# A 2-D FFT and maxout layer: stage one's result turned by VectorE's 32x32 transposition instead of by a way through DRAM

## The chip, the cores and the metric

One core of a Trainium2 chip. The metric is the device time of one launch in microseconds (us). The inputs and the output are float32 in DRAM; the kernel's matmuls take bfloat16.

## The reference

```
x: (8, 3072, 256)             # 8 images
X = fft(x, axis=1); X = fft(X, axis=2); a = X.real          # (8, 3072, 256)
t = a.reshape(24576, 256)
h = max(t @ w1, t @ w2, t @ w3)                             # w1..w3: (256, 768)
out = h @ w_out                                             # w_out: (768, 256)
```

The real part of a 2-D FFT of a real image has a symmetry: row k and row 3072-k hold the same values with the second axis reversed. The kernel computes "even" and "odd" parts (`tE`, `tO`) for half of the rows and gets one row of each pair from their sum and the other from their difference. The second axis' DFT is folded into the weights: `gE`, `gO`, `gD` are products of w1 to w3 with tables of cosines and sines, made on the chip at the start.

## The kernel before

**Stage one** (`s`, L365). An image lies in `xt` as 49 residues s of the row index. 13 matmuls per image multiply it by a small table `tab`; seven evictions, mostly by ACT (L372, L376), put the result into `tb`: a partition is an output row of stage one (64 of them, two s in the two halves), and a residue's 128 columns lie side by side.

**The turn.** Stage two needs the residues on the partitions. `y` (L378) writes `tb` to a DRAM buffer `db`, and `z` (L388) reads it back as `yb`, 98 rows (two for each residue). Both go by SP's DMA queue. `u` (L393), `x0` (L396) and `c` (L403) make one extra column of `yb` from the image's first column.

**Stage two** (`k`, L406). 32 small matmuls an image multiply `yb` with the tables `te_tab` and `to_tab`; each group of 512 columns is evicted as a third of `tE` or `tO` (L413). The tables are sines of angles that VectorE reduces and ACT evaluates, in three parts of about 512 columns (`angle`, `table`).

**The units.** An image has 18 units: 3 blocks of 512 tokens times 6 slices of 128 hidden columns. A unit's `begin` makes the sum rows and its `finish`, one unit later, the difference rows. There are two kinds. In the plain kind (even units, and the first few odd ones) PE makes two products for the sum (L436, L437), ACT takes the relu of one bank (L450, `stmp`), VectorE the maximum with the other (L451, `hp`); then PE adds the difference product into the same banks (L444), and ACT and VectorE do the same again (`hm`). In the split kind (odd units from the seventh on) only one bank is kept: PE (L772, L773) and VectorE's maximum (L774, `hp`) with `plus3`, then PE's L444 and VectorE's L786 (`hm`) with `minus3`. `third` makes `plus3` and `minus3` a unit or more ahead: PE L756 and L758, ACT L760 (`odd`), VectorE L761 (`even`), POOL L765.

**The second layer** (`l2_block`, L464) runs ten steps a unit from a queue: matmuls into `po` (L460, L483), VectorE's add (L488, `ot`), stores by SP (L496) and by POOL's indirect DMA (L570).

**What sets the order.** All engines' queues are written by hand: instructions stand on each engine in program order. `plan` maps (image, unit) to a list of pieces, which stand at the end of that unit, after `l2_some(10)`. `ahead0` (image 0) and `ahead` (the others) say in which units the next image's pieces stand: the stage-one matmuls, `y`, `z`, `x`, `c`, and the groups `kE0` to `kO2`. Loads and mirrorings (`mirror`, L129, L131; `mirror_first`, L136) of images two ahead are in the same plan. PSUM: three banks for `ps_f`, two for `pse2`, one for `pse3`, two for `po`; a larger pool `ps_s` takes their place in the start.

**The start.** While image 0 arrives in four pieces, PE runs warm-up matmuls and stage one as far as it has data. Then come the weight products for the first three slices (`product`, L296: 16 matmuls of 384 columns), image 0's first stage-two groups, and unit 0. The weights come in six loads (`load_w`), three of them before the images and three after `z`.

Of the kernel before, what the change touches and what calls it, by code (L numbers as in the profile page):

```python
# [11 lines left out]
INT32 = mybir.dt.int32  # L12
AX = mybir.ActivationFunctionType
ALU = mybir.AluOpType

ROUND = 12582912.0
# [34 lines left out]
def kernel(  # L51
# [20 lines left out]
    KS = 2 * NS  # L72
# [8 lines left out]
    dbs = [d_pool.tile([NS, 4 * RI * 128], BF16, name=f"db{i}", tag=f"db{i}") for i in range(2)]  # L81
# [9 lines left out]
    x0u = consts.tile([128, KS + 1], BF16, tag="x0u")  # L91
    ybv = yb.rearrange("p (r e f) -> p r e f", e=2, f=128)
# [13 lines left out]
    gE = [consts.tile([128, DFF], BF16, name=f"gE{i}", tag=f"gE{i}") for i in range(2)]  # L106
    gO = [consts.tile([128, DFF], BF16, name=f"gO{i}", tag=f"gO{i}") for i in range(2)]
    gD = [consts.tile([128, DFF], BF16, name=f"gD{i}", tag=f"gD{i}") for i in range(2)]
# [41 lines left out]
    ang_r = gen.tile([128, 4 * RI], FP32, tag="ang_r")  # L150
    iota(ang_r, [[0, 4], [1, RI]], base=1)
    iota(ang_r.rearrange("p (g r) -> p g r", r=RI)[:, :, 15:17], [[0, 4], [16, 2]])
# [9 lines left out]
    def load_w(jh, after=None):  # L162
        for wsrc, wdst in ((moe_w1, w1_bf), (moe_w2, w2_bf), (moe_w3, w3_bf)):
            ld = nc.gpsimd.dma_start(
                out=wdst.rearrange("p (fc j) -> p fc j", fc=2)[:, :, jh * 384:(jh + 1) * 384],
                in_=wsrc.rearrange("(fc p) j -> p fc j", fc=2)[:, :, jh * 384:(jh + 1) * 384])
            if after is not None:
                tc.add_manual_dep(ld.ins, after.ins.name, AFTER, reason="others first")

    load_w(0)  # L170
# [3 lines left out]
    for r in (0, 6, 11):  # L174
        n = {0: 6, 6: 5, 11: 4}[r]
        iota(kv[:, r:r + n, :], [[1, n], [32, 96]], base=r + 1)
    iota(kvec[:, 1408:1504].rearrange("p (r j) -> p r j", r=2), [[16, 2], [32, 48]])
# [3 lines left out]
    rows_f = gen.tile([128, 12 * B], FP32, tag="rows_f")  # L181
    iota(rows_f.rearrange("p (b t u) -> p b t u", t=4, u=3), [[S, B], [-4, 4], [-1025, 3]],
         base=S - 1, cm=-32)
    zero = gen.tile([128, 512], BF16, tag="zero")
    nc.vector.memset(zero, 0.0)
    for db in dbs:
        pads = db[:, 64 * 128:].rearrange("s (r c) -> s r c", c=256)
        nc.sync.dma_start(out=pads, in_=zero[0:NS].rearrange("p (r c) -> p r c", c=256))
# [5 lines left out]
    ang_o = gen.tile([128, 4 * RI], FP32, tag="ang_o")  # L194
    nc.vector.memset(ang_o, 0.0)
    nc.vector.memset(ang_o[:, 0:RI], 8.0)
    nc.vector.memset(ang_o[:, 3 * RI:4 * RI], 24.0)
# [3 lines left out]
    def scal(out, in0, s1, op0, s2=None, op1=None, eng=None):  # L201
# [3 lines left out]

    up, sidx, hflag, alpha, sig, sgm = (small(n) for n in
                                        ("up", "sidx", "hflag", "alpha", "sig", "sgm"))
    scal(up, pidx, 64.0, ALU.is_ge)
    nc.vector.scalar_tensor_tensor(out=sidx, in0=up, scalar=-64.0, in1=pidx,
                                   op0=ALU.mult, op1=ALU.add)  # L210
    scal(hflag, sidx, 32.0, ALU.is_ge)
    scal(alpha, sidx, -2.0, ALU.mult, 31.0, ALU.add)
    nc.vector.scalar_tensor_tensor(out=alpha, in0=alpha, scalar=hflag, in1=sidx,
                                   op0=ALU.mult, op1=ALU.add)
# [3 lines left out]
    ang_q = gen.tile([128, 4 * RI], FP32, tag="ang_q")  # L218
# [4 lines left out]
    nc.vector.tensor_copy(out=tab[:, 0:64:2], in_=ang_q[:, 0:32])  # L223
    scal(tab[:, 1:64:2], ang_q[:, 0:32], sig, ALU.mult)
    scal(tabx, ang_q[:, 2 * RI:4 * RI], sgm, ALU.mult)

    dve = nc.vector.tensor_copy
    half = gen.tile([128, 256], FP32, tag="half")
    nc.vector.memset(half[:, 0:128], 64.0)
# [632 lines left out]
```

## Time and profile before

| | |
|---|---|
| median of 3 runs | 400.75 us (400.54 to 400.95) |
| the profiled execution: its own time, and its span | 400.15 us, 397.9 us |
| PE, DVE, ACT, POOL busy | 96%, 80%, 65%, 82% of the span |
| instructions of PE, DVE, ACT, POOL in the profile | 2739, 542, 466, 408 |
| DMA packets, bytes | 69532, 56.30 MB |
| granted TensorE clock | full, but for 14.0 to 20.8 us, where it was half |
| one image in the steady state | 45 us, 18 units |

How to read it: busy shares are means over stages with different limits. The first 40 us are the start, with PE idle in places; from there the table by windows gives PE as busy for 48.00 of 48 us. The lines of the profile are quoted with the prediction. In them DVE is VectorE, ACT is ScalarE, POOL is GpSimd, SP is SyncE, PE is TensorE's matmul and PEld its weight load; a duration that the timeline gives for one instruction overlaps with the next one's where instructions are pipelined, so the distance between starts can be shorter. `L774` is line 774 of the kernel before.

### The profile page before, as it was taken

The numbers are of one execution on the slowest core, as the hardware profiler recorded it, in microseconds if no ns is written. First come the engines' busy times: TensorE is split into PE (matmuls) and PEld (weight loads), VectorE is DVE, ScalarE is ACT, GpSimd is POOL, SyncE is SP. The second block draws the span as 40 slices with busy tenths as digits, with TensorE's granted clock in tenths as the row PEclk, the third lists the DMA queues.
The fourth block names the chain that finished last, engine by engine and source line by source line (L and its number), as shares of the span: only waits on it lengthen the run. The fifth ranks groups of instructions, "written<-read, shape, count | busy, mean of one in ns | idle before, by whom it ended". The sixth has DMA issues, their size and how long they took to land.

```text
span 397.9 us, 8345 instructions
## 1 busy us (share of the span) xinstructions
PE 382.8 (96%) x2739; PEld 236.3 (59%) x2739; DVE 317.6 (80%) x542; ACT 259.6 (65%) x466; POOL 324.6 (82%) x408
## 2 busy tenths in 40 slices
PE   7598999999999999999999999999999999999994
PEld 2254466656665666666665666666665666666673
DVE  6977797877887887877887887877887887887982
ACT  2577689768856788568866788568766547544420
POOL 7376389879988899889988899889878798879993
PEclk9799999999999999999999999999999999999999
DMA  8989987494776777395776877394432563322234
GB/s 121 196 175 195 167 229 147 122 192 145 141 154 123 177 165 162 108 190 148 147 155 117 183 166 153 108 200 127 129 112 82 133 154 104 91 77 50 88 88 138
DMA packets 69532, 56.30 MB, mean 141 GB/s; under 512 B 35040, under 2 KB 64992, under 8 KB 68292
## 3 DMA queue, kind: packets, MB, share of 16 engines
q0 software_dynamic: 23552, 26.53, 35.9%
q1 hardware_dynamic: 44898, 28.70, 28.1%
q10 hardware_dynamic: 1040, 0.56, 0.5%
q8 instruction: 21, 0.34, 0.4%
q14 instruction: 21, 0.17, 0.1%
HBM read 38.15 MB, written 31.71 MB: 176 GB/s over the span
## 4 chain that ended last, share of the span: by engine, by line
PE 86%; DMA 6%; ACT 3%; DVE 2%; POOL 1%; issue 1%; SPq 0%; POOLq 0%; DVEq 0%; ACTq 0%
PE po L460 30%; PE pse L444 11%; PE pse L436 7%; PE pse L437 7%; PE po L483 5%; PE pse L772 4%; PE pse L773 4%; PE e L756 4%; PE d L758 4%; PE ps L369 3%; DMA yb<-db 3%; PE ps L411 3%; PE pl L475 2%; DMA xt<-in_x_dram 2%; ACT stmp L450 1%; POOL xt L122 1%
## 5 line engine op out<-in xcount | busy, mean ns | idle before, releaser
L450 ACT ACTIVATE stmp<-pse 128x512 bf16<-128x512 f32 x150 | 89.6, 600 | 64.0 <-PE pse L444 39.8
L570 POOL DMA_INDIRECT out_dram<-ot,rows_m x92 | 102.3, 1112 | 17.9 <-issue 7.5
L765 POOL TENSOR_TENSOR plus<-even,odd 128x512 bf16<-128x512 f32 x69 | 87.9, 1274 | 34.0 <-DVE even L761 26.9
L765 POOL TENSOR_TENSOR minus<-even,odd 128x512 bf16<-128x512 f32 x69 | 87.6, 1270 | 0.0
L460 PE MATMUL po<-wout_bf,hp 128*128 128x256 bf16 x576 | 86.1, 273 | 0.0
L774 DVE SCALAR_TENSOR_TENSOR hp<-pse,plus 128x512 bf16<-128x512 f32 x69 | 47.6, 689 | 46.7 <-PE pse L773 26.2
L460 PE MATMUL po<-wout_bf,hm 128*128 128x256 bf16 x576 | 78.6, 273 | 0.0
L460 PEld LDWEIGHTS <-hp 128*128 128x128 bf16 x576 | 56.4, 98 | 26.1
L444 PE MATMUL pse<-tO,gD 128*128 128x512 bf16 x219 | 70.9, 379 | 0.0
L460 PEld LDWEIGHTS <-hm 128*128 128x128 bf16 x576 | 56.4, 98 | 16.3
L488 DVE TENSOR_TENSOR ot<-po,even 128x512 f32<-128x512 f32 x92 | 62.6, 681 | 0.0
L451 DVE TENSOR_TENSOR hp<-pse,stmp 128x512 bf16<-128x512 f32 x75 | 51.4, 685 | 10.8 <-ACT stmp L450 9.4
L436 PE MATMUL pse<-tE,gE 128*128 128x512 bf16 x150 | 56.8, 378 | 2.0 <-DVE hm L451 0.7
L451 DVE TENSOR_TENSOR hm<-pse,stmp 128x512 bf16<-128x512 f32 x75 | 51.5, 687 | 7.1 <-ACT stmp L450 3.9
L437 PE MATMUL pse<-tO,gO 128*128 128x512 bf16 x150 | 56.8, 379 | 0.0
L761 DVE SCALAR_TENSOR_TENSOR even<-vb,wcol,e 128x512 f32<-128x512 bf16 x69 | 50.8, 737 | 0.0
L786 DVE SCALAR_TENSOR_TENSOR hm<-pse,minus 128x512 bf16<-128x512 f32 x69 | 47.0, 681 | 0.9 <-PE pse L437 0.3
L760 ACT ACTIVATE odd<-d 128x512 f32<-128x512 f32 x69 | 41.3, 598 | 6.6 <-POOL minus L765 0.4
L129 ACT COPY xt<-xt 64x762 bf16<-64x762 bf16 (+1 forms) x48 | 40.2, 838 | 1.1
L372 ACT CAST tb<-ps 128x512 bf16<-128x512 f32 x46 | 24.8, 589 | 21.5 <-PE ps L369 21.5
L444 PEld LDWEIGHTS <-gD 128*128 128x128 bf16 x219 | 21.4, 98 | 23.1 <-issue 5.0
L483 PE MATMUL po<-gw,tO 128*128 128x512 bf16 x92 | 34.9, 380 | 0.0
(156 smaller groups left out, 468.3 us busy)
## 6 DMA issues: line engine op xcount, KB each, us to landing
yb<-db SPq DMA_DIRECT2D x7, 833.0 KB
xt<-in_x_dram POOLq DMA_DIRECT2D x14, 384.0 KB, 9.2
out_dram<-ot SPq DMA_DIRECT2D x55, 96.0 KB
out_dram<-ot SPq DMA_DIRECT2D x64, 64.0 KB
db<-tb SPq DMA_DIRECT2D x21, 192.0 KB
vb<-vd SPq DMA_DIRECT2D x23, 128.0 KB
xt<-in_x_dram POOLq DMA_DIRECT2D x7, 400.0 KB, 7.3
xt<-in_x_dram POOLq DMA_DIRECT2D x7, 368.0 KB
```

What stands on the lines that cost most here:

```text
L436: nc.tensor.matmul(pse[:, 0:n], gE[i][:, js], te, start=True, stop=False)
L437: nc.tensor.matmul(pse[:, 0:n], gO[i][:, js], to, start=False, stop=True)
L444: nc.tensor.matmul(pse, gD[i][:, js], to, start=False, stop=True, skip_group_check=True)
L450: nc.scalar.activation(out=stmp[:, 0:n], in_=pses[0][:, 0:n], func=AX.Relu)
L451: nc.vector.tensor_tensor(out=dst, in0=src3, in1=stmp[:, 0:n], op=ALU.max)
L460: nc.tensor.matmul(po, hcols(jc), wout_bf[:, jc * 256:(jc + 1) * 256], start=False, stop=(jc == NJC - 1), skip_group_check=True)
L483: nc.tensor.matmul(po, to[:, cp], gw[:, 256:768], start=True, stop=True)
L488: nc.vector.tensor_tensor(out=ot.rearrange("p (h c) -> p h c", h=2), in0=po.rearrange("p (h c) -> p h c", h=2), in1=lin.unsqueeze(1).to_br ...
L570: stored(nc.gpsimd.indirect_dma_start(out, bass.IndirectOffsetOnAxis(ap=rows_m[0:128 - lo, at_row: at_row + 1], axis=0), ot[lo:128, 256:51 ...
L761: nc.vector.scalar_tensor_tensor(out=even3, in0=vb, scalar=wcol[:, jc:jc + 1], in1=e3, op0=ALU.mult, op1=ALU.add)
L765: nc.gpsimd.tensor_tensor(out=dst, in0=even3, in1=odd3, op=op)
L774: nc.vector.scalar_tensor_tensor(out=dst, in0=pse2, scalar=0.0, in1=sums[g][0], op0=ALU.max, op1=ALU.max)
```

## The change

- **The turn.** `tb` becomes a tile of 32-bit words, each a pair of bf16 columns, with 64 pairs x 32 residue slots. ACT's evictions write pairs 128 bytes apart. `t` transposes blocks of 32x32 words on VectorE from `tb` into `yb`, whose words of one residue slot lie 256 bytes apart when written: image 0 in one instruction of 128x64x32, the others in four of 128x16x32 (`t0` to `t3`). `y`, `z`, the DRAM buffers and their padding are gone.
- **Rows renumbered.** The turn gives each quadrant of 32 partitions 16 rows of `yb`; stage two uses 17. The seventeenth comes out in the sixteenth row of the neighbouring quadrant, and `f` puts it right, twice (for two pairs of quadrants): ACT copies 32 x 256 bf16 across, and VectorE's memset clears the place that it came from. Stage two's matmuls take 128 rows for 98 (unused residue slots are zero).
- **The extra column.** `x0` writes `yb` directly for images 1 to 7, so `c` is used for image 0 alone, in parts; `u` is two copies on POOL for one.
- **The plan.** `ahead0`: `t0` to `t3` at units 8 to 11, `f` behind `t3`, `x` at 12. `ahead`: `t0` to `t3` at units 4, 6, 8, 10, `f` behind `t3`, `x` at 11.
- **The start.** The first weights come in three loads of 128 columns and three of 256; the last three no longer wait for `z`. The first products are 16 matmuls of 128 columns in one bank and 16 of 256 columns in two banks, before 16 of 384; one eviction takes a bank. Part of the angle reduction goes from VectorE to ACT (`turns`) and POOL, and the tables 512:1024 move to units 0 and 1 of the plan.

```diff
-    tb = consts.tile([128, 25 * 128], BF16, tag="tb")
-    tbv = tb.rearrange("p (s f) -> p s f", f=128)
-    yb = consts.tile([128, 2 * RI * 128], BF16, tag="yb")
+    tb = consts.tile([128, 64 * 32], UINT32, tag="tb")
+    tbw = tb.rearrange("p (f s) -> p f s", s=32)
+    tbv = tb.bitcast(BF16).rearrange("p (f s l) -> p f s l", s=32, l=2)
+    yb = consts.tile([128, 2 * RI * 64], UINT32, tag="yb")
+    ybw = yb.rearrange("p (q f) -> p q f", f=64)
+    ybv = yb.bitcast(BF16).rearrange("p (r e f) -> p r e f", e=2, f=128)
...
-    load_w(0)
...
+    load_w(0, 0, 128)
+    ramp(0)
+    load_w(1, 0, 128)
+    ramp(6)
+    load_w(2, 0, 128)
+    for k in range(3):
+        load_w(k, 128, 384)
...
+    def turns(q, v, per):
+        nc.scalar.activation(out=q, in_=v, func=AX.Identity, scale=1.0 / per, bias=rnd[:, 0:1])
+        nc.scalar.activation(out=q, in_=q, func=AX.Identity, scale=1.0, bias=rnd[:, 1:2])
...
-                evict(out=tb[:, k * 512:(k + 1) * 512], in_=ps1)
+                evict(out=tbv[:, :, 4 * k:4 * k + 4, :],
+                      in_=ps1.rearrange("p (s f l) -> p f s l", s=4, l=2))
...
-        def y(self, s0=0, s1=NS, second=nc.sync):
...
-        def z(self, i0=0, i1=RI, s0=0, s1=NS):
...
+        def t(self, f0=0, f1=64):
+            nc.vector.transpose(out=ybw[:, 0:32, f0:f1].rearrange("p q f -> p f q"),
+                                in_=tbw[:, f0:f1, :])
+
+        def f(self):
+            for a in (0, 64):
+                nc.scalar.copy(out=ybv[a:a + 32, 16], in_=ybv[a + 32:a + 64, 15])
+                nc.vector.memset(ybw[a + 32:a + 64, 30:32, :], 0)
...
-            nc.scalar.copy(out=x0s[0:KS, :], in_=psx[0:KS, 0:RI])
+            nc.scalar.copy(out=out, in_=psx[:, 0:RI])
...
-                nc.tensor.matmul(ps2[:, c0:c0 + wd], ybv[0:KS, i, which, :],
-                                 tab[0:KS, g * 512 + c0:g * 512 + c0 + wd], start=True, stop=True)
+                nc.tensor.matmul(ps2[:, c0:c0 + wd], ybv[:, i, which, :],
+                                 tab[:, g * 512 + c0:g * 512 + c0 + wd], start=True, stop=True)
...
     m.s(4, pool=ps_s)
-    m.s(5, pool=ps_s)
+    table(0, 0, 512)
+    m.s(5, pool=ps_s, evict=dve)
     m.s(6, pool=ps_s)
-    m.y(32, NS, nc.scalar)
...
+    m.t()
     m.u()
-    m.x0()
-    tables(0, 512)
-    m.z(0, 6, 0, 32)
...
+    m.x0(x0s)
+    table(1, 0, 512)
+    psg0 = products(ps_f, 0, 2, 0, 128)
+    keep(psg0, 0, 2, 0, 128, nc.scalar.copy)
+    table(2, 0, 512)
+    for k in range(3):
+        load_w(k, 384, 768)
...
+    psg1 = products(ps_s, 0, 1, 128, 384)
     warm_up(2)
+    psg2 = products(ps_s, 1, 2, 128, 384)
+    m.c(0, 6)
+    differ(0, 2, 0, 128)
     m.k(0, 0, dve)
-    keep_product(psg, 1, 1, 0, dve)
-    m.c(0, 6, nc.scalar.copy)
     m.k(1, 0)
-    table(2, 512, 1024)
...
-    for (u, fn) in ((0, lambda: next(second)), (0, lambda: m.c(6, RI, nc.scalar.copy)),
+    for (u, fn) in ((0, lambda: wrap(512, 1024)), (0, lambda: next(second)),
+                    (0, lambda: m.c(6, 15)), (0, lambda: differ(0, 2, 128, 384)),
+                    (0, lambda: table(1, 512, 1024)), (0, lambda: table(2, 512, 1024)),
+                    (1, lambda: table(0, 512, 1024)), (2, m.f), (2, lambda: m.c(15, RI)),
...
-    ahead = {1: ("s0", "s1"), 2: ("s2", "y0", "s3", "s6"), 3: ("s4", "s5", "y1", "u"), 5: ("x",),
-             7: ("z",), 11: ("c",), 12: ("kO0",), 13: ("v0", "kE0", "kO1"), 14: ("v1", "kE1"),
-             15: ("kO2",), 16: ("v2", "kE2", "end")}
+    ahead = {1: ("s0", "s1"), 2: ("s2", "s3", "s6"), 3: ("s4", "s5", "u"), 4: ("t0",), 6: ("t1",),
+             8: ("t2",), 10: ("t3", "f"), 11: ("x",), 12: ("kO0",), 13: ("v0", "kE0", "kO1"),
+             14: ("v1", "kE1"), 15: ("kO2",), 16: ("v2", "kE2", "end")}
```

More of the change, by code (lines that the diff above doesn't have):

```diff
@@ L12 @@
 INT32 = mybir.dt.int32
+UINT32 = mybir.dt.uint32
 AX = mybir.ActivationFunctionType
@@ L270, in angle @@
             nc.vector.tensor_tensor(out=kvec[:, cs], in0=kvec[:, cs], in1=q[:, cs], op=ALU.add)
-    def angles(c0, c1):
-        for part in range(2):
-            angle(part, c0, c1)
     def table(k, c0=1024, c1=NHALF + 1):
@@ L284, in table, with product @@
                                  bias=half_pi)
-    def tables(c0, c1):
-        for k in range(3):
-            table(k, c0, c1)
-    def product(i, half, jh, pool, tag):
-        psg = pool.tile([128, 512], FP32, name="psg", tag=tag)
+    def product(psg, c, i, half, j0, j1):
         hs = slice(half * 128, (half + 1) * 128)
@@ L315, in prep_first @@
             for half in range(2):
-                keep_product(product(i, half, 1, ps_f, "ps"), i, half, 1, nc.vector.tensor_copy)
+                psg = ps_f.tile([128, 512], FP32, name="psg", tag="ps")
+                product(psg, 0, i, half, 384, 768)
+                (nc.vector.tensor_copy, nc.scalar.copy)[half](
+                    out=g_all[:, 2 * i + half, 384:768], in_=psg[:, 0:384])
+                if half:
+                    differ(i, i + 1, 384, 768)
                 yield
@@ L406, in k, with c @@
+        def c(self, i0=0, i1=RI):
+            nc.scalar.copy(out=ybv[:, i0:i1, 1, 0], in_=x0s[:, i0:i1])
         def k(self, which, g, evict=nc.scalar.copy):
@@ L599 @@
     m.s(1, pool=ps_s)
-    m.y(0, 16)
     warm_up(5)
```

212 lines of the change are left out of this document (105 added, 107 removed).

## The prediction

> **What bounds the kernel now.** First the page's busy rows and slices.
>
> ```profile
> PE 382.8 (96%) x2739; PEld 236.3 (59%) x2739; DVE 317.6 (80%) x542; ACT 259.6 (65%) x466; POOL 324.6 (82%) x408
> PE   7598999999999999999999999999999999999994
> PEclk9799999999999999999999999999999999999999
> ```
>
> PE is full from slice 4 (about 40 us) to the last. The table by windows makes it exact:
>
> ```profile
> 22.30:42.00 19.70, 17.55 (x150) 9.99 (x151) 15.01 (x28) 13.40 (x29) 13.99 (x25) 1.00 1.10 175
> 90.00:138.00 48.00, 48.00 (x347) 30.01 (x345) 38.73 (x62) 35.66 (x64) 42.43 (x51) 1.00 0.69 148
> 186.00:234.00 48.00, 48.00 (x347) 29.94 (x345) 38.84 (x61) 35.97 (x63) 42.54 (x50) 1.00 0.72 155
> ```
>
> (columns: window, its length, busy PE, PEld, DVE, ACT, POOL, clock, DMA). PE's waits after 42 us are three, 0.9 us in all, none on the way through DRAM: L411, which reads `yb`, waits there 0.2 us, for ACT. So for images 1 to 7 the DRAM way is hidden, and removing it can't gain. It is seen only for image 0, in the chain of waits:
>
> ```profile
> 15.46 3.71 DMA db<-tb
> 19.52 2.63 DMA yb<-db
> 22.28 0.40 PE ps L411 x6
> ```
>
> Yet PE itself waited only 0.34 us there: until 21.9 it ran the weight products (L296) and the warm-ups, half of them at half clock (granted 0.5 from 14.0 to 20.8, two steps of 3.4).
>
> The steady state then hangs on slack. VectorE and ACT are each other's and PE's partners in every unit; this is the place that decides (an odd unit's `hp`, L774, in image 3; the same gap within 0.02 us in images 1 to 6):
>
> ```profile
> 189.91 0.68 DVE L451 TENSOR_TENSOR hp<-pse,stmp 128x512 bf16<-128x512 f32 x1
> 190.51 0.68 DVE L488 TENSOR_TENSOR ot<-po,even 128x512 f32<-128x512 f32 x1
> 191.11 0.68 DVE L774 SCALAR_TENSOR_TENSOR hp<-pse,plus 128x512 bf16<-128x512 f32 x1
> 191.71 0.68 DVE L451 TENSOR_TENSOR hm<-pse,stmp 128x512 bf16<-128x512 f32 x1
> 192.22 0.82 ACT L129 COPY xt<-xt 64x762 bf16<-64x762 bf16 x1
> 192.43 0.38 PE L444 MATMUL pse<-tO,gD 128*128 128x512 bf16 x1
> ```
>
> L444 adds into the bank that L774 reads, so it can't begin before L774 ends, 191.79: slack 0.64. On VectorE, steps of 512 follow each other every 0.60 us.
>
> **Start-up, part by part.** (1) Image 0's two DMAs leave the path: 3.71 + 2.63 and their issue (15.28 to 22.28) go. In their place: mirrors and the stage-one eviction to about 15.9, small VectorE steps, one transposition of 2,048 words a partition. At VectorE's contiguous f32 rate (512 elements every 0.60) that is some 2.2 us, 16.75 to about 19.0; at double, to 21.1. (2) PE's own queue is next late: s5, s6 and psx to 15.85, psg0 (16 matmuls of 128 columns at half clock, 0.107 each by L296's 0.32 for 384) to 17.55, psg1 to 19.26, two warm-ups to 20.1, psg2 to 21.3. So k starts near 21.35 in place of 22.28: -0.9, whether the transposition takes 2.2 or 4.4. PE's stage-one work is the same and 16 more short matmuls cost 0.1. The narrower loads cost 0: the chain shows no weight load, and PE has stage one to run until 15.85; each us that the first one lands later than that would cost one. The SP queue loses 42 issues that PE never waited for. (3) Back comes ACT's order. The 512:1024 tables now stand in unit 0, after unit 0's relu and before unit 1's:
>
> ```profile
> 23.44 0.72 ACT L283 ACTIVATE to_tab<-q,half_pi 128x512 bf16<-128x512 f32 x1
> 24.71 0.69 DVE L451 TENSOR_TENSOR hp<-pse,stmp 128x512 bf16<-128x512 f32 x1 [1.08 <-ACT stmp L450]
> 26.01 0.69 DVE L451 TENSOR_TENSOR hp<-pse,stmp 128x512 bf16<-128x512 f32 x1
> ```
>
> Before, unit 1's hp starts 2.56 after unit 0's first matmul (23.45). After: hp (0.60), `wrap` (0.70), |angle| (0.61), to_tab (0.72), unit 1's relu (0.60) follow each other across the two engines, 4.45: +1.9, with `f` and `c` of image 0 +0.2; PE has nothing else to do there (17.55 of 19.7). Start in all: -0.9 + 2.1 = +1.2 (bounds -0.7 if the clock rises one 3.4 us window earlier and the tables hide, +1.4 without that).
>
> **Steady state.** (4) y, z (33 + 11 DMAs) and `c` removed: 0, hidden now. PE in k: 128 rows for 98, same columns: 0. (5) Added per image: four chunks of 512 words, at 0.60 each, in units 4, 6, 8, 10. VectorE's 38.8 of 48 (36.4 of an image's 45.15) becomes 39: room in the mean. t0, t1 and t2 stand ahead of L774 of units 5, 7, 9, which have idle time plus slack of 1.1, 1.7, 1.6: 0. (6) t3 and `f` stand in unit 10, exactly ahead of the L774 shown, where VectorE has no idle time. `f` is copy (ACT), memset (VectorE), copy, memset: the copies wait for t3, each memset for its copy, and L774 and hm (L451) queue behind the memsets. t3 191.11 to 191.80; a copy of 256 on ACT, 0.185 + 256 x 0.84 ns by the slope of L129's two lengths = 0.40: first to 192.2, second to 192.6; memset to 192.7; L774 192.74 to 193.43. L444 192.43 becomes 193.46: PE stalls 1.03 us, with no other work in its queue ahead of that matmul. Six images (2 to 7): 6.2 us. (7) For image 1 the pieces lie in units 8 to 11 of image 0: t1 and t2 are 1.2 ahead of unit 11's L774 with about 1.0 of room: 0.25; t3 and `f` stand before `ot` and before hm (L786, 58.72), which frees the bank for unit 13's matmul at 59.93; t3, both copies and the memsets take about 1.9 more: 1.7 of it stalls. Together 2.0.
>
> **The unknown: strided words.** Evictions now write bf16 pairs 128 bytes apart, the transposition words 256 bytes apart; the trace has neither. Lower bound: contiguous price, 0.589 an eviction and 0.60 a chunk. Upper bound, from ACT's copies to bf16 at 512 bytes' stride:
>
> ```profile
> L404 ACT COPY yb<-x0s 98x17 bf16<-98x17 bf16 x7 | 1.9, 265 | 1.1 <-DMA yb<-db 1.0
> L136 ACT COPY xt<-xt 64x49 bf16<-64x49 bf16 x6 | 2.5, 409 | 0.1
> ```
>
> 32 elements more cost 0.144: 4.5 ns an element for 0.84 contiguous. At 4.5 a pair, an eviction is 1.33 us, and 12 of them put ACT from 33.6 to 42.5 of 45.15 us an image. At 4.5 a word a chunk is 2.4 us, VectorE 46.6 of 45.15: bound by VectorE. I take the contiguous price, as whole 4-byte words are nearer to the f32 rows of VectorE than to single bf16; both ends stay for the range. [...]
>
> **Sum**, against the profiled execution's 400.15: +1.2 + 2.0 + 6.2 = 409.5. The median of the runs is 0.6 above it: 410.1, said as 410.
>
> **Rivals.**
> A, strided words cost double or more (slower still). At 1.2 a chunk t0 to t2 eat the slack of units 5, 7 and 9 and t3 adds 0.55: about 2.0 an image for 1.03, image 1 3 us: near 417. If instead ACT's pairs cost 1.33, some 2 us an image more: 423. Both: about 430; the full 4.5 ns on VectorE, beyond 440. For it: the two ACT rows; against: they are 2-byte elements. Chance 0.32. [...]
> B, `f` is hidden (the copies are so short that the chain ends by 192.43): then only the start is left, 400.75 + 1.2, about 402. Against: the order of the queues and the slack of 0.64. Chance 0.10.
> C, faster: the start gains and nothing is given back. It needs the 512:1024 tables to hide beside PE's L411 and products, and a chain of t3 and `f` below 0.64 us. Then k at 21.35 or, if the clock is back by 17.4, at 19.5: -0.9 to -2.5, 398.3 to 399.9. For it: all DMA is off image 0's path; against: unit 0's ACT queue has 1.3 us put in it. It holds from the point where L774 of unit 11 ends by 192.43. Chance 0.10.
> D, no difference: gains and losses cancel. Chance 0.02.
> The forecast, 406 to 413 alone: 0.46.
>
> The range leaves out most of C, half of B and A's upper quarter: 402 to 427. About 0.2% (0.8 us) is what a measurement of this kernel can tell from no change; faster 0.10, same 0.02, slower 0.88.
>
> **What would show it.** Right: PE waits at L444 in units 11 of images 1 to 6, each about 1 us, for DVE hp; two small memsets ahead of it on VectorE, waiting for ACT's yb copies; transposition rows of 0.65 to 0.7 us; tb evictions near 0.59; k(0,0) near 21.4; unit 1's hp 4.4 after unit 0's first matmul. Wrong: PE still 48.00 of 48 in every window; chunk or eviction rows of 1.2 us and more, which make A; PE waits at e or `po` for POOL or ACT, which I have not priced.

## The result and the profile after

The changed kernel takes 421.31 us (median of 6 runs, 419.83 to 423.23); the kernel before, run beside it, 400.64. Ratio 1.052, 95% interval 1.0486 to 1.0548: slower by 20.7 us, where +9.3 was forecast. The profiled execution took 422.2 us with a span of 420.4 (before: 400.15 and 397.9).

The page's busy rows and slices of the kernel after:

```profile
PE 388.8 (92%) x2755; PEld 239.3 (57%) x2755; DVE 348.8 (83%) x588; ACT 265.5 (63%) x478; POOL 330.9 (79%) x422
...
PE   7668997999899998999899998999899998999994
PEclk9698998999999999999999999999999999999999
```

The row of 9s of before is broken by an 8 about every image, and slices 2, 3 and 7 are low (a slice is 10.5 us). The table by windows of the kernel after (columns as before: window, length, PE, PEld, DVE, ACT, POOL, clock, DMA):

```profile
90.00:138.00 48.00, 46.16 (x332) 28.50 (x332) 40.33 (x63) 33.85 (x61) 40.50 (x49) 1.00 0.51 109
186.00:234.00 48.00, 46.18 (x333) 28.81 (x332) 41.10 (x66) 34.30 (x62) 40.41 (x49) 1.00 0.52 109
```

PE, 48.00 of 48 before, now lacks 1.8 in each. No other engine is full, so it waits for steps in an order.

The loss by stage follows from two kinds of marks in PE's timeline: the first `psw` matmul (end of the start) and the one-column matmul that closes stage two of each image.

| stage | before | after | loss |
|---|---|---|---|
| to `psw` | 38.83 | 43.58 | 4.75 |
| to the end of image 1's stage two | 34.06 | 38.87 | 4.81 |
| the next six images, to the last mark | 267.31 | 280.02 | 12.71 |
| of these, one image in the steady state | 44.88 | 47.06 | 2.18 |

The three losses make 22.3 of the 22.5 by which the spans differ. The medians differ by less, 20.7, as the profiled execution of the kernel after is 0.9 above its median and that of before 0.5 below its own.

Two of these losses hang in part on the execution that was profiled. Three kernels of the experiments (the one without `f` and the first two plans) have the same code up to `psw`, and theirs stands at 42.50 to 43.46: the start loses 3.7 to 4.75. And 1.7 of image 1's 4.81 is a stretch at half clock that four kernels with the same work in image 1 don't show (below).

**The new instructions.** The groups by shape of the kernel after (count, busy, mean ns of one, idle before it):

```profile
L415 DVE STREAM_TRANSPOSE yb<-tb 128x512 uint32<-128x512 uint32 x28 | 29.6, 1057 | 0.0
L415 DVE STREAM_TRANSPOSE yb<-tb 128x2048 uint32<-128x2048 uint32 x1 | 3.7, 3724 | 0.1
L406 ACT CAST tb<-ps 128x512 bf16<-128x512 f32 x45 | 24.3, 588 | 16.5 <-PE ps L403 16.5
L420 ACT COPY yb<-yb 32x256 bf16<-32x256 bf16 x16 | 6.4, 402 | 16.8 <-DVE yb L415 16.6
L421 DVE MEMSET yb<- 32x128 uint32 x16 | 2.6, 165 | 5.6 <-ACT yb L420 2.9 <-issue 2.6
```

A chunk takes 1.06 us, and its successor starts 0.91 us behind it (190.47 to 191.38 below), not 0.60: 1.74 ns a word (the difference of the two lengths over 1,536 words). The pair-wise eviction costs what the contiguous one did (588 ns, before 589), and `f`'s copy the 0.40 that was worked out.

**An odd unit 11.** The timeline of the kernel after in image 3 (start, duration; in brackets idle time and its releaser), the place that the prediction showed for before:

```profile
205.55 1.05 DVE L415 STREAM_TRANSPOSE yb<-tb 128x512 uint32<-128x512 uint32 x1
...
206.64 0.83 ACT L420 COPY yb<-yb 32x256 bf16<-32x256 bf16 x2 [2.31 <-DVE yb L415]
...
207.12 0.17 DVE L421 MEMSET yb<- 32x128 uint32 x1 [0.52 <-ACT yb L420]
...
207.55 0.17 DVE L421 MEMSET yb<- 32x128 uint32 x1 [0.26 <-issue]
207.74 0.69 DVE L808 SCALAR_TENSOR_TENSOR hp<-pse,plus 128x512 bf16<-128x512 f32 x1
...
208.49 0.38 PE L476 MATMUL pse<-tO,gd_all 128*128 128x512 bf16 x1 [1.41 <-DVE hp L808]
```

(L808 is before's L774, L476 its L444.) t3, copy, memset, copy, memset, L808, L476 stand in the order forecast. From the start of t3 to that of L808 it is 2.19 us; the prediction's steps give 1.63. PE's wait is 1.41 as the profile counts it, from the modelled end of the matmul ahead.

**Unit 9**, in which the prediction put no stall. The same timeline from unit 4's t0 on:

```profile
190.47 1.06 DVE L415 STREAM_TRANSPOSE yb<-tb 128x512 uint32<-128x512 uint32 x1
...
192.56 0.72 DVE L795 SCALAR_TENSOR_TENSOR even<-vb,wcol,e 128x512 f32<-128x512 bf16 x1
...
193.43 1.27 POOL L799 TENSOR_TENSOR plus<-even,odd 128x512 bf16<-128x512 f32 x1 [1.51 <-DVE even L795]
...
197.37 2.56 POOL L602 DMA_INDIRECT out_dram<-ot,rows_m  x1 [0.21 <-issue]
...
199.98 1.28 POOL L799 TENSOR_TENSOR plus<-even,odd 128x512 bf16<-128x512 f32 x1
...
201.30 0.69 DVE L808 SCALAR_TENSOR_TENSOR hp<-pse,plus 128x512 bf16<-128x512 f32 x1 [0.70 <-POOL plus L799]
...
202.04 0.38 PE L476 MATMUL pse<-tO,gd_all 128*128 128x512 bf16 x1 [0.40 <-DVE hp L808]
```

Each of these steps is compared with the same step of the kernel before, whose timeline has

```profile
178.11 0.74 DVE L761 SCALAR_TENSOR_TENSOR even<-vb,wcol,e 128x512 f32<-128x512 bf16 x1
...
185.54 1.27 POOL L765 TENSOR_TENSOR plus<-even,odd 128x512 bf16<-128x512 f32 x1
...
186.85 0.69 DVE L774 SCALAR_TENSOR_TENSOR hp<-pse,plus 128x512 bf16<-128x512 f32 x1 [1.59 <-POOL plus L765]
...
187.60 0.38 PE L444 MATMUL pse<-tO,gD 128*128 128x512 bf16 x1
```

PE's matmul ahead of it (L806 of unit 7, before's L772) is 13.89 us later than before (194.54 for 180.65). But `even` is later by 14.45 (178.11 before), the first `plus` by 14.43 (179.00), the second by 14.44 (185.54), L808 by 14.45 (186.85), L476 by 14.44 (187.60). So t0 puts VectorE 0.56 us behind PE, POOL's first `plus` waits for `even` and then has no room: `plus`, `minus`, two scatters and the next `plus` follow each other until 201.3. The 1.59 us in which VectorE was idle before L774 there were a wait for this chain; PE had no slack at its end (L774 at 186.85 ended 0.06 before L444 began). t1 (195.01) and t2 (199.54) stand in idle time of units 7 and 9, and no step that PE waits for begins behind them: they cost nothing.

From unit 9 to unit 11 the shift grows to 16.06 (L476 at 208.49, before's L444 at 192.43). So unit 9 loses 0.55 and unit 11 1.62, the 2.17 of an image's 2.18.

**Image 1.** The table of PE's waits of the kernel after, from 46 to 400 us (sum, times, longest):

```profile
PE pse L476 <- DVE hp L808: 11.0, 12, 1.4
...
PE pse L806 <- DVE hm L820: 2.6, 2, 2.3
```

The twelve are those of units 9 and 11 in images 2 to 7. The two on L806 belong to image 1's pieces: 0.27 at 60.49 and 2.30 at 67.83, where `hm` stands behind t3, `f` and `ot`, as step 7 said. The long one leaves 1.10 us of PE work in a window of 3.4 us, and the next one runs at half clock. The table by windows of the kernel after, in the start and here:

```profile
27.00:30.40 3.40, 1.79 (x14) 0.90 (x13) 2.33 (x6) 3.16 (x6) 3.03 (x8) 1.00 1.51 238
30.40:33.80 3.40, 3.35 (x15) 1.66 (x15) 3.32 (x5) 2.05 (x5) 3.40 (x6) 0.54 1.28 175
...
64.60:68.00 3.40, 1.10 (x11) 0.81 (x9) 2.59 (x6) 2.54 (x5) 3.25 (x3) 1.00 0.35 64
68.00:71.40 3.40, 3.40 (x13) 1.75 (x12) 2.41 (x4) 2.08 (x5) 2.39 (x6) 0.53 0.73 126
```

In the window at half clock PE's matmuls of 512 columns start 0.43 us apart (L790 at 69.13, L792 at 69.56), at full clock 0.22 (L468 at 63.81, L469 at 64.03), so 3.4 us there do 1.7 us of work: about 1.7 of image 1's 4.81 is this. The runs bear it out: the kernels with the evictions on ACT, with the angle step moved, with the start's new order and with the first plan have the same work in image 1 and no half clock there, and take 37.17 to 37.19 us for it, 1.7 less than 38.87. The gap in front is the same (the two waits sum to 2.6 in each), so the window at half clock is in part luck: in steps of 3.41 us counted from the clock's changes, the gap lies in one step here and is shared by two with the angle step moved (lines with that experiment). The other 3.1 are the change's.

**The start.** The timeline of the kernel after:

```profile
18.45 3.72 DVE L415 STREAM_TRANSPOSE yb<-tb 128x2048 uint32<-128x2048 uint32 x1
...
22.23 0.40 PE L443 MATMUL ps<-te_tab,yb 128*128 128x96 bf16 x6 [0.39 <-DVE yb L415]
...
23.27 1.28 DVE L333 CAST g_all<-psg 128x512 bf16<-128x512 f32 x2
...
24.61 0.39 PE L468 MATMUL pse<-tE,g_all 128*128 128x512 bf16 x1 [1.73 <-DVE g_all L333]
...
30.91 1.19 DVE L212 TENSOR_SCALAR kvec<-kvec,s_of,phi 128x513 f32<-128x513 f32 x1
```

The transposition begins at 18.45, not 16.75, and takes 3.72, so k(0,0) stands at 22.23, where it stood before (22.28): nothing gained in this execution. VectorE's last mirroring of image 0 ends at 16.12 here, behind angle steps and a memset, and at 13.96 before; in the three kernels with the same code up to `psw` k(0,0) stands at 21.17 to 22.09. VectorE's evictions of the products come behind it, so unit 0's first matmul (L468) is at 24.61 for 23.45, and unit 1's `hp` at 29.10 for 26.01. Then VectorE's angle step (L212) takes 1.19, which was 0.54 before; POOL is at its mirror copies at that time (28.70 to 31.8; before they began at 34.29). The half-clock window above follows.

### The profile page after: what moved, and what is told of

It reads as the page before. It is cut to its first block, busy times and chain, and to the rows that moved or that the text cites. A ratio compares the mean times of both kernels' runs of the same rounds, so it can differ in the third digit from the quotient of the medians.

```text
span 420.4 us, 8330 instructions
## 1 busy us (share of the span) xinstructions
PE 388.8 (92%) x2755; PEld 239.3 (57%) x2755; DVE 348.8 (83%) x588; ACT 265.5 (63%) x478; POOL 330.9 (79%) x422
## 4 chain that ended last, share of the span: by engine, by line
PE 62%; DVE 16%; issue 9%; POOL 8%; ACT 2%; DMA 1%; DVEq 0%; POOLq 0%; ACTq 0%
PE po L492 21%; PE pse L476 9%; PE pse L468 5%; PE pse L469 5%; PE po L515 3%; PE pse L806 3%; POOL plus L799 3%; DVE hm L483 3%; POOL out_dram L602 3%; PE pse L807 3%; PE ps L403 3%; DVE yb L415 3%; PE ps L443 2%; PE d L792 2%; PE e L790 2%
## 5 line engine op out<-in xcount | busy, mean ns | idle before, releaser
L476 PE MATMUL pse<-tO,gd_all 128*128 128x512 bf16 x219 | 71.7, 384 | 11.1 <-DVE hp L808 11.0
L808 DVE SCALAR_TENSOR_TENSOR hp<-pse,plus 128x512 bf16<-128x512 f32 x69 | 47.4, 686 | 31.6 <-PE pse L807 18.1
L483 DVE TENSOR_TENSOR hp<-pse,stmp 128x512 bf16<-128x512 f32 x75 | 51.3, 684 | 12.4 <-ACT stmp L482 11.4
L468 PE MATMUL pse<-tE,g_all 128*128 128x512 bf16 x150 | 56.8, 379 | 3.5 <-DVE g_all L333 1.7
L469 PE MATMUL pse<-tO,g_all 128*128 128x512 bf16 x150 | 57.0, 380 | 0.0
L476 PEld LDWEIGHTS <-gd_all 128*128 128x128 bf16 x219 | 21.4, 98 | 23.2 <-issue 5.3
```

The lines of the kernel that those rows point to most:

```text
L468: nc.tensor.matmul(pse[:, 0:n], gE[i][:, js], te, start=True, stop=False)
L469: nc.tensor.matmul(pse[:, 0:n], gO[i][:, js], to, start=False, stop=True)
L476: nc.tensor.matmul(pse, gD[i][:, js], to, start=False, stop=True, skip_group_check=True)
L483: nc.vector.tensor_tensor(out=dst, in0=src3, in1=stmp[:, 0:n], op=ALU.max)
L808: nc.vector.scalar_tensor_tensor(out=dst, in0=pse2, scalar=0.0, in1=sums[g][0], op0=ALU.max, op1=ALU.max)
```

## The experiments

The theory: (a) words 256 bytes apart cost 1.74 ns each, which makes the chunks long; (b) t3 and `f` hold up L808 of unit 11; (c) the chunks put VectorE late, which reaches PE through POOL's `plus` in unit 9; (d) the start's 4.75 is VectorE's order. The rivals: the stalls come from the mere presence of chunks, from the new order of ACT's tables, or from other waits that the profile puts down to L808.

Short words, all else the same. `yb`'s words are written side by side, so stage two reads other data:

```diff
-            nc.vector.transpose(out=ybw[:, 0:32, f0:f1].rearrange("p q f -> p f q"),
+            nc.vector.transpose(out=yb[:, 0:2048].rearrange("p (f q) -> p f q", q=32)[:, f0:f1, :],
```

> The changed kernel with the transposition's output words side by side instead of 256 bytes apart (the words then lie at wrong places; same number of words, same plan). Theory (the words' distance costs): the chunk of 512 words falls from 1.06 us to about 0.68, image 0's 2,048 words from 3.72 to about 2.2. Then t1 fits into the 0.70 us that VectorE is idle ahead of unit 7 and the wait in unit 9 (0.57 us by the start of L476) is gone, and the one in unit 11 falls from 1.58 to about 1.1: 2.18 an image becomes 1.0 to 1.2, which is what the prediction had; with image 1 some -7 to -8: 413 to 414.5. Rival (a transposition of 32-bit words takes two cycles a word wherever it writes): rows stay at 1.06 and the time at 421.

416.00 us, ratio 1.038 (1.0347 to 1.0413). The groups of this kernel:

```profile
L415 DVE STREAM_TRANSPOSE yb<-tb 128x512 uint32<-128x512 uint32 x28 | 19.6, 701 | 0.0
L415 DVE STREAM_TRANSPOSE yb<-tb 128x2048 uint32<-128x2048 uint32 x1 | 2.3, 2311 | 0.1
```

The same words cost 1.05 ns each when written side by side, 1.74 when 256 bytes apart. The image goes from 47.06 to 46.41: the words' distance is worth 0.65 an image, and 5.3 us in all by the medians (4.3 by the profiled spans). Unit 9's wait falls from 0.40 to 0.16, unit 11's from 1.41 to 1.07: both hang on the chunk's length. The forecast's own price for a chunk (0.60 between starts) was this kernel's (0.62). Even so an image loses 1.53 against before, more than the 1.0 to 1.2 expected here and than the 1.03 of the forecast.

Without `f` (the seventeenth row of `yb` is not put right in images 1 to 7):

```diff
-            mm.f()
+            pass
```

> The changed kernel without f (the two ACT copies and two VectorE memsets) for images 1 to 7; the 17th row is left out there. Theory (t3 and f together hold L808 of unit 11): the wait in unit 11 falls from 1.58 us to about 0.4 (t3 alone, 1.0 for 0.64 of slack), unit 9's 0.57 stays: images 2 to 7 gain 6 x 1.15 = 6.9; image 1's 2.3 us wait at unit 13 loses about 1 us, and with a gap shorter than a clock window the half-speed window behind it (1.7 us) goes too: about 411 to 412.5. Rival (the long transposition holds the queue by itself, f runs in its shadow): within 1 us of 421.

410.85 us, ratio 1.0257 (1.0219 to 1.0294); the image 45.75, so `f` costs 1.31. Unit 11's wait is gone, unit 9's is left, 0.4 each in six images. The windows of image 1 in this kernel:

```profile
64.60:68.00 3.40, 2.37 (x17) 1.44 (x17) 3.17 (x6) 2.24 (x5) 3.24 (x5) 1.00 0.32 82
68.00:71.40 3.40, 3.40 (x39) 2.45 (x37) 2.40 (x4) 3.09 (x6) 3.10 (x5) 1.00 0.94 130
```

With 2.37 us of PE work in the first, the second keeps its full clock, and image 1 falls from 38.87 to 35.86. Of these 3.01, 1.70 is the half-clock window, which kernels that keep `f` lack too (37.17); `f` itself costs 1.31 there, as in any other image.

Both together:

> The changed kernel with words side by side (at wrong places) and without f for images 1 to 7 (17th row left out): t0 to t3 alone, at the price that the prediction took. Theory (steps 5 and 6 of the prediction: at 0.7 a chunk the four fit into idle time and slack, all the rest is f): period 44.9 to 45.2 us, 405 to 407 with the start's 4.7. Rival (four chunks cost even at that price): period 45.4 or more.

406.75 us, ratio 1.016 (1.0115 to 1.0204). The image is 45.14 to 45.16. The four kernels make a table, us an image (before: 44.88):

| | words side by side | 256 bytes apart |
|---|---|---|
| without `f` | 45.15 | 45.75 |
| with `f` | 46.41 | 47.06 |

The terms add: `f` 1.26 or 1.31, the distance 0.60 or 0.65, and 0.27 for the chunks' presence and whatever else the change brings. So step 5's "0 stall" was nearly right at the price that it assumed.

The start. Its evictions of the products on ACT, ahead of the transposition's end:

```diff
+    keep(psg1, 0, 1, 128, 384, nc.scalar.copy)
+    keep(psg2, 1, 2, 128, 384, nc.scalar.copy)
     m.c(0, 6)
...
-    keep(psg1, 0, 1, 128, 384, dve)
-    keep(psg2, 1, 2, 128, 384, dve)
```

> The changed kernel with the two evictions of the 256-column products on ACT (idle 20.0 to 22.2 us) instead of on VectorE behind the long transposition. Theory (unit 0's first matmul waits for PSUM banks that these evictions free): L468 of unit 0 starts near 23.4 instead of 24.6, and most of that is kept: 420 to 420.5. Rival (the wait is for tE and g_all anyway, or unit 1's relu takes it back): 421.3, no difference.

421.89 us, ratio 1.0544 (1.0516 to 1.0572): no gain. The first matmul of unit 0 comes 1.19 us behind k(0,0), for 2.38 in the kernel after, but then the angle steps meet POOL's copies: `q` on 128x513 takes 1.70 us. What was gained is given back: from k(0,0) to `psw` it is 21.11, for 21.35. This theory of the start fell.

The tables 512:1024 out of unit 0:

```diff
-                    (0, lambda: table(1, 512, 1024)), (0, lambda: table(2, 512, 1024)),
+                    (1, lambda: table(1, 512, 1024)), (1, lambda: table(2, 512, 1024)),
...
-                    (1, lambda: m.k(1, 1)), (1, lambda: next(second)), (1, lambda: angle(0)),
-                    (2, lambda: m.v(1)), (2, lambda: m.k(0, 1)),
+                    (1, lambda: next(second)), (1, lambda: angle(0)),
+                    (2, lambda: m.k(1, 1)), (2, lambda: m.k(0, 1)), (2, lambda: m.v(1)),
```

> The changed kernel with the three tables 512:1024 behind unit 1's relu instead of ahead of it, and their first users (kO1, kE1, v1) in unit 2. Theory (wrap, |angle|, to_tab stand between unit 0's and unit 1's maximum, and the PE gap that they make, 1.85 busy of 3.5 us, costs a half-speed window behind it): unit 1's maximum starts 1.9 us earlier and the window from 30.5 to 34 us keeps the full clock: -2.5 to -3.6, 417.7 to 418.8. Rival (PE then waits at kO1 for to_tab instead, the gap only moves): -0.5 or less, 420.8 to 421.3.

423.02 us, ratio 1.0558 (1.0515 to 1.0601): no gain again. Unit 1's `hp` did come earlier, 26.90 for 29.10; 1.15 of it is the edit's (3.34 us behind unit 0's first matmul for 4.49), the rest is this execution's earlier start. The timeline of this kernel tells what took its place:

```profile
29.49 1.45 POOL L134 COPY xt<-xt 64x1524 bf16<-64x1524 bf16 x1
29.53 1.70 DVE L212 TENSOR_SCALAR q<-kvec 128x513 f32<-128x513 f32 x1
...
33.55 0.80 PE L319 MATMUL psg<-w_bf,md_all 128*128 128x384 bf16 x2 [3.18 <-DVE g_all L347]
```

VectorE's `q`, 0.43 in the kernel before, starts with POOL's copy and takes 1.70; the evictions of products behind it free PE's banks late, PE waits 3.18, and the clock is half from 32.5 to 39.4. `q` ends 0.29 us after the copy (31.23 for 30.94).

The angle step moved ahead of POOL's copies, alone:

```diff
-                    (1, lambda: m.k(1, 1)), (1, lambda: next(second)), (1, lambda: angle(0)),
+                    (1, lambda: m.k(1, 1)), (1, lambda: next(second)), (0, lambda: angle(0)),
```

> The changed kernel with the third part's first two VectorE steps (513 columns) in unit 0, ahead of POOL's mirror copies of image 1, instead of in unit 1, beside them. Theory (VectorE's scaling steps take 1.2 to 1.7 us for 0.54 and 0.43 while POOL copies, and hold unit 2's maximum): both rows back to 0.54 and 0.43, unit 2's maximum about 1 us earlier, -1 to -2: 419.3 to 420.3. Rival (the start is held by ACT's tables): no difference, 421.

419.44 us, ratio 1.046 (1.0427 to 1.0492): 1.9 less than the kernel after, with intervals that still overlap. The timeline of this kernel:

```profile
27.16 0.54 DVE L212 TENSOR_SCALAR kvec<-kvec,s_of,phi 128x513 f32<-128x513 f32 x1
27.48 1.63 POOL L134 COPY xt<-xt 64x1651 bf16<-64x1651 bf16 x1
27.73 1.67 DVE L212 TENSOR_SCALAR q<-kvec 128x513 f32<-128x513 f32 x1
```

The step that begins before the copy takes its old 0.54, the next one, 0.25 us after the copy's start, 1.67; it too ends 0.29 behind the copy. This edit moves one group of VectorE steps and nothing else; but POOL's copy came earlier too, so the collision was not removed. Nor does the profile show that the 1.9 is the edit's: from k(0,0) to `psw` it is 21.32 us, for 21.35 in the kernel after. What differs is image 1, 37.17 for 38.87, whose code is the same. This kernel's windows there:

```profile
64.60:68.00 3.40, 1.08 (x5) 0.54 (x6) 2.65 (x6) 3.05 (x7) 3.25 (x5) 1.00 0.32 78
68.00:71.40 3.40, 3.40 (x30) 2.40 (x29) 3.19 (x6) 3.22 (x6) 2.67 (x5) 1.00 0.98 129
```

With no more PE work in the first (1.08, 1.10 in the kernel after) the second is at full clock. The clock changes at 30.68 and 68.22 us in the kernel after, eleven steps of 3.41 apart, and at 14.1 and 20.9 in this one; counted on from there, the gap lies in one step there (64.8 to 68.2, 1.11 us of PE work) and is shared by two here (65.3 to 68.7 has 1.81).

The start as a whole: the memsets of `tb` and `yb` and a sign column earlier, evictions on ACT, tables in unit 1, the angles a unit later, `f` in unit 3:

```diff
+    nc.vector.memset(tbw[:, :, 24:32], 0)
...
+    keep(psg1, 0, 1, 128, 384, nc.scalar.copy)
+    keep(psg2, 1, 2, 128, 384, nc.scalar.copy)
...
+                    (1, lambda: next(second)), (2, lambda: angle(0)),
...
+                    (2, lambda: next(first)), (2, lambda: next(first)), (3, lambda: angle(1)),
```

> The changed kernel with only the start's order mended as in e7_best; steady state as in the changed kernel. Theory: -3.5 to -5, 416.5 to 418. Rival (given back by unit 5): 420 or more.

420.37 us, ratio 1.049 (1.045 to 1.0529): 0.9 less than the kernel after, no more than the spread of the runs. `kvec` and `q` (28.51, 1.09 us, and 29.64, 1.70 us) fall upon POOL's copies again.

The plan of images 2 to 7 (the stage-one pieces two units earlier, which needs the tiles of an image to be taken later; image 1 as it was):

```diff
-    ahead = {1: ("s0", "s1"), 2: ("s2", "s3", "s6"), 3: ("s4", "s5", "u"), 4: ("t0",), 6: ("t1",),
-             8: ("t2",), 10: ("t3", "f"), 11: ("x",), 12: ("kO0",), 13: ("v0", "kE0", "kO1"),
+    ahead = {-1: ("s0", "s1"), 0: ("s2", "s3", "s6"), 1: ("s4", "s5", "u"), 2: ("t0-24",),
+             4: ("t24-40",), 8: ("t40-64",), 10: ("f",), 11: ("x",), 12: ("kO0",),
```

> The changed kernel with other places for the work of images 2 to 7: stage one two units earlier, the transposition in three chunks of 24, 16 and 24 columns at units 2, 4 and 8 (about 1.55, 1.06, 1.55 us), f alone at unit 10, its copies no longer behind a transposition. Theory (the losses of the steady state are a matter of place: t1 ahead of POOL's scatter, and t3 with f ahead of L808 of unit 11): the waits at L476, 0.57 and 1.58 an image by the starts, go to below 0.3 together: 6 x 1.9 = -11, about 409.5 to 411. Rival 1 (VectorE has no room for 4.2 us more an image wherever it lies): still over 1.5 an image, 418 or more. Rival 2 (stage two's 128 rows or the strided words cost PE itself): the period stays above 46.5 us with no waits shown.

412.95 us, ratio 1.0312 (1.027 to 1.0355); the image 45.88. With t out of unit 10, `f` stands there alone and unit 11's wait is gone: it was the chain from t3 through `f` to L808, not `f` as such. What is left is unit 9's wait of 0.4, more than expected. A chunk still stands in unit 4, and the chain from `even` through POOL to `plus` is the one shown above.

The same for image 1 (`f` in unit 14, its column through `c` in parts):

```diff
-    ahead0 = {5: ("s0", "s1"), 6: ("s2", "s3"), 7: ("s4", "s5", "s6", "u"), 8: ("t0",),
-              9: ("t1",), 10: ("t2",), 11: ("t3", "f"), 12: ("x",), 13: ("kO0",),
+    ahead0 = {5: ("s0", "s1"), 6: ("s2", "s3"), 7: ("s4", "s5", "s6", "u"), 8: ("t0-24",),
+              10: ("t24-40",), 11: ("X",), 12: ("t40-64",), 13: ("C",), 14: ("kO0", "f"),
+              15: ("v0", "kE0", "kO1", "D"), 16: ("v1", "kE1"), 17: ("kO2",),
```

> As e5_plan, and image 1's transposition in chunks of 24, 16, 24 at units 8, 10, 12 of image 0, its extra column and f apart from them, its stage two one unit later. Theory (image 1 lost 0.3 + 2.3 us of waits and, because the gap emptied most of a clock window, 1.7 us at half clock behind it): no wait above 0.5 at unit 13, PEclk 1.00 in 68 to 71.4 us: -3.5 to -4.5 against e5_plan, about 405.5 to 407. Rival (the half-speed window comes whatever the gap): -2.5 or less.

412.40 us, ratio 1.0282 (1.0243 to 1.0321). The wait before unit 13 is gone and the clock is full from 42 to 90 us, but against the plan of images 2 to 7 alone it is only 0.5. From `psw` to the end of image 2's stage two the gain is 1.4 (81.19 to 79.79); the start came out 1.0 longer in this profiled execution (43.46 for 42.50), though its code is the same. The expectation was too high for a reason that the profile shows: the half-clock window of image 1 was already absent in the profiled execution of the plan of images 2 to 7 alone (37.19 to the end of image 1's stage two, 38.87 in the kernel after), so its 1.7 us were counted twice. The 1.0 of the start arose before anything that the edit moves: VectorE's last mirroring of image 0 began at 15.82 for 14.90. So single executions differ by more than the 0.5, and what the edit is worth between 0.5 and 1.4 is not settled.

This plan with the start:

> As e6_plan01, with the start's order mended: VectorE's memsets and the sign column early, the 256-column products evicted by ACT, the 512:1024 tables and kO1, kE1 behind unit 1's relu, the third part's angles a unit later, after POOL's mirror copies. Theory (the start's 4.7 us are queue order on VectorE and ACT and the half-clock windows that PE's gaps bring): the transposition starts near 17.7 for 18.45, unit 0's first matmul near 23.1 for 24.6, no half-clock window after 21: -3.5 to -5 against e6_plan01: 401 to 403, about the kernel before. Rival (PE has too little to do there, so the time is given back by unit 5): -1.5 or less, 404.5 to 406.

412.95 us, ratio 1.0301 (1.0261 to 1.0342): no better. k(0,0) came at 20.83, but `psw` at 42.53; `q` at 29.43 beside POOL's copy of 29.01 took 1.56.

The same with the angles a unit earlier, `angle(0)` in unit 1 and `angle(1)` in unit 2, `f` in unit 2, and a plan of its own for image 2, pieces of the others up to four units ahead:

```diff
+                    (1, lambda: table(0, 512, 1024)), (1, lambda: angle(0)),
...
+    ahead1 = {-1: ("s0", "s1"), 0: ("s2", "s3", "s6"), 1: ("s4", "s5", "u"), 2: ("t0-32",),
+              8: ("t32-64",), 10: ("f",), 11: ("x",), 12: ("kO0",),
...
+    ahead = {-4: ("s0",), -3: ("s1", "s2"), -2: ("s3", "s6"), -1: ("s4", "s5", "u"), 0: ("t0-16",),
+             2: ("t16-40",), 8: ("t40-64",), 10: ("f",), 11: ("x",), 12: ("kO0",),
```

> All places mended: as e7_best, but images 3 to 7 have stage one three units earlier again and the transposition at units 0, 2 and 8 (16, 24, 24 columns; none at unit 4, where e5_plan left 1.0 an image), image 2 at units 2 and 8; the third part's angles stay ahead of POOL's mirror copies. Theory (nothing but places is lost): the period comes down from 45.88 to 44.9 to 45.1 us, the first of the layer's psw matmuls from 42.5 to near 39.5: 400 to 404. If the start's lead (stage two of image 0 at 20.8 for 22.3) is kept, 399. Rival (VectorE's 4.2 us more an image push POOL's additions wherever they lie): period above 45.5, 406 or more.

408.54 us, ratio 1.0193 (1.0166 to 1.0221). `psw` is at 39.57, 0.74 behind the kernel before. The window of this kernel that had 1.79 us of PE in the kernel after:

```profile
27.00:30.40 3.40, 3.03 (x27) 1.92 (x27) 3.37 (x7) 2.60 (x6) 3.20 (x5) 1.00 1.31 216
```

`q` (27.77) is back at 0.43, and no window of this execution is at half clock. PE's and VectorE's marks of the start, us (the third column has the kernel without `f` and the first two plans, whose code is the same up to `psw`):

| | before | after | same start | this version |
|---|---|---|---|---|
| k(0,0) at | 22.28 | 22.23 | 21.17 to 22.09 | 21.33 |
| from there to unit 0's first matmul | 1.17 | 2.38 | 2.37 to 2.39 | 1.19 |
| to unit 1's `hp` | 2.56 | 4.49 | 4.50 | 3.35 |
| to unit 2's `hp` | 2.77 | 3.37 | 3.06 to 3.36 | 2.85 |
| to `psw` | 10.05 | 11.11 | 11.10 to 11.12 | 10.85 |

So the change puts 1.2 us on the way by VectorE's evictions behind the transposition, 1.9 with the tables in unit 0 (1.1 of it goes when they stand in unit 1), 0.3 to 0.6 by the angle step (`kvec` takes 0.88 where it is 0.3, 1.17 to 1.19 where it is 0.6), and 1.1 behind that, whose cause is open. The half-clock window from 30.68 on in the kernel after cost nothing up to `psw`: the three others have none there and the same distances. This version takes back 2.9 to 4.0 us of the start's 3.7 to 4.75; so (d) holds, with the tables and POOL's copies beside VectorE's order. Its image is 45.72, above the 44.9 to 45.1 expected: neither wait of units 9 and 11 is left, but PE waits 0.3 us an image for a PSUM bank of stage one that ACT frees; the rest of the 0.84 above before lies in no single wait.

The last: as this one, with the plan `ahead1` for all images, two chunks of 1,024 words an image in units 2 and 8:

```diff
+    ahead = {-1: ("s0", "s1"), 0: ("s2", "s3", "s6"), 1: ("s4", "s5", "u"), 2: ("t0-32",),
+             8: ("t32-64",), 10: ("f",), 11: ("x",), 12: ("kO0",),
```

> As e9_best, with stage one of images 2 to 7 at the places of e5_plan (the unit before the image's first, and its first two) and the transposition in two chunks of 32 columns at units 2 and 8 (about 2.05 us each). Theory (e9_best's remaining 0.84 us an image are PE's waits for PSUM banks behind stage one at the crowded units 15 to 17; unit 2 and unit 8 have about 3.0 and 1.6 us of room): period 45.2 to 45.5, 405.5 to 407.5. Rival (POOL's additions of unit 9 are held by any chunk ahead of them): period 45.8 or more, 408.5 or more. Either way above the kernel before's 400.6: the start's lead is spent on the tables, and VectorE's added work has no counterpart that PE waited for.

406.85 us, ratio 1.0161 (1.0136 to 1.0187). The window of this kernel in image 3:

```profile
186.00:234.00 48.00, 47.60 (x336) 29.29 (x341) 42.25 (x65) 36.06 (x63) 42.01 (x52) 1.00 0.51 110
```

The image is 45.44, and neither wait of units 9 and 11 is left in the steady state, though a chunk takes 1.94 us: no chunk stands in unit 4, ahead of unit 6's `even`, and none right before `f`. With the version before it, which has no chunk in unit 4 either, and the first plan, which has one there and the 0.4, that settles (c). Of the 20.7 us lost, 14 are back without touching what the change does; it is the fastest version found that computes the same result, and still 1.6% behind the kernel before. Against that one it loses 0.8 to `psw`, 3.5 to the end of image 2's stage two and 0.56 in each image after.

## Why the prediction was partly right

Right: the sign, and why. The way through DRAM was hidden for images 1 to 7 and its removal gained nothing (4); t3 and `f` ahead of unit 11's L774 were the largest stall (6), in the order that was written out; the pair-wise eviction was free; the two bounds of the words held the truth. The time lies in the range, and rival A's upper half (417 to 423) is where it came out, but there by luck: A's 423 rested on ACT's pairs, which cost nothing, and its 417 on lost slack in units 5, 7 and 9, of which unit 9 alone lost any, through POOL. What lifted the time above 417 was the start and a half-clock window.

The size was wrong: in the profiled executions the steady state lost 6.5 us more than forecast, image 1 2.8 and the start 3.6. Five terms failed:

- **The price of strided words** ("I take the contiguous price"): this was the choice that failed, and the largest error. Measured 1.74 ns a word, 1.06 us a chunk (0.91 between starts); with short words 5.3 us by the medians, 4.3 by the profiled spans, of the 11.4 by which the loss exceeds the forecast are gone. Rival A had the right kind of price; ACT's 4.5 ns an element was far above it. (The upper bound for ACT also counts 12 evictions an image where the kernel has seven; at its price ACT would have come to about 38 us, not 42.5. The forecast doesn't rest on it.) The pairs paid nothing (588 ns for 589), the single words did (1.74 against 1.05 ns); the price taken, 0.60 us for 512 words (1.17 ns each), fits the words side by side alone (0.62 between starts, 1.05 ns a word).
- **Step 6**, 1.03 us in unit 11: 1.62. The copies begin 1.09 after t3's start, not 0.69, which is 0.40 of the difference; the gaps between copies and memsets make most of the rest.
- **Step 5**, no stall for t0 to t2: 0.55 in unit 9. Its room of 1.6 there was VectorE's idle time in front of L774, which was a wait for POOL's chain; t2 fits into it, but t0, two units ahead of that chain's start, makes the chain late. The prediction's last lines name a wait for POOL as one that it had not priced.
- **Step 7**, 2.0 for image 1: 4.81. Its waits for `hm` were named and came (0.27 and 2.30). A half-clock window behind them, in part luck, added 1.7; of the other 3.1 the words' price makes about 1.0, an estimate: with short words image 1 took 37.90 with such a window, so some 36.2 without, 2.1 above before.
- **Steps 1 to 3**, +1.2 for the start: +4.75, or 3.7 and 4.6 in other executions of the same code. k at 21.35 was no error: it came at 21.17 to 22.23. Nor was the way from unit 0's first matmul to unit 1's `hp`, 4.45: it came out at 4.49. What is next late was sought on PE and ACT, and VectorE's queue was left out: its evictions behind the transposition (1.2), and the angle step beside POOL's copies (0.3 to 0.6). The 0.2 for the rest of the start was 1.1. Moving the tables out of unit 0 alone gained nothing, as `q` then fell upon POOL's copy; with the angles ahead of the copies it did.

Open: what the 1.1 us ahead of `psw` are, and what the angle's move alone is worth; and what remains of 0.56 an image in the last version, where no single wait carries it.

## What to carry to other kernels

Follow a step that is put into a tight order beyond the next wait of its own engine: to the slowest queue that it feeds (here POOL's) and back. Price a strided write by a row of its own; a price that no row shows moves every step behind it, here 0.65 us in each image. Before work is moved into an engine's idle time, ask what that time waits for, and before it is moved out of a full stage, whom it meets in the next: the first edits of the start gave back nearly all they had gained. And before a difference of 1 or 2 us is given to an edit, look whether the stages that the edit leaves alone are the same in both profiles: here the start moved by up to 1.1 us, and image 1, with or without a half-clock window, by 1.7, with the same code.

## What the runs showed of the hardware

- VectorE's transposition of 32-bit words: 1.05 ns a word when written side by side, 1.74 when 256 bytes apart; ACT's bf16 pairs 128 bytes apart cost nothing extra (588 against 589 ns for 128x512).
- VectorE's scaling steps (`kvec`, `q`) on 128x513 float32 from SBUF to SBUF took 0.42 to 0.54 us in the kernel before, where POOL's copies come later, and up to 1.70 beside a POOL copy of bf16; where one began under such a copy and outlasted it, it ended 0.28 to 0.29 us behind it (31.23 for 30.94 with the tables out of unit 0, 29.40 for 29.11 with the angle step moved, 32.10 for 31.81 in the kernel after, 29.60 for 29.32 with the start's new order). Maxima and evictions with an operand in PSUM kept their 0.68 beside the same copies (0.67 to 0.68 at 29.32, 29.92 and 30.52 with the angle step moved, beside the copy of 29.40 to 30.85).
- In the first 100 us the clock changed at 13.61, 20.44, 30.68, 34.09, 68.22 and 71.64 us in the kernel after, at distances of 3.41 us and its multiples, and at 14.00 and 20.82 in the kernel before. In steps of 3.41 us counted from these points, half clock came behind 0.95 us of PE work (ahead of 13.61), 1.76 (ahead of 30.68) and 1.11 (ahead of 68.22) in the kernel after, and behind 1.05 (ahead of 14.00) in the kernel before; full clock stayed behind 1.81 with the angle step moved (at 65.3) and behind 2.04 in the kernel after (at 20.44). What amount of work divides the two was not shown.
